# Weight loads in 4 KB source runs, and one packet per transfer and engine, in a fused attention and spectral-mixing kernel

## The chip, the cores and the metric

The kernel runs on one core of one Trainium2 chip. The metric is device time in microseconds (us) of one execution. The kernel before takes 456.14 us, the median of three runs (455.82 to 456.61). The profiled execution has a span of 453.8 us.

## The reference: what is computed

The program is a causal attention followed by a mixing of the sequence's lowest 64 frequencies. Cut to what matters:

```python
# attention: q, k, v are (8 batches, 8 heads, 576 positions, 64), s is (8, 8, 576)
cum    = cumsum(maximum(s, 0), axis=-1)
scores = q @ k.T / 8 + minimum(-(cum[..., :, None] - cum[..., None, :]), 0)   # causal
x      = softmax(scores) @ v                       # as (8, 576, 512)

# spectral mixing: w_r, w_i are (64 modes, 512, 512), w_ch is (512, 512)
X  = rfft(x, axis=1)[:, :64]                       # 64 modes of 512 channels, complex
Yr = einsum('bmd,mde->bme', X.real, w_r) - einsum('bmd,mde->bme', X.imag, w_i)
Yi = einsum('bmd,mde->bme', X.real, w_i) + einsum('bmd,mde->bme', X.imag, w_r)
u  = x + irfft(Yr + 1j * Yi, n=576)
out = u + maximum(u @ w_ch, 0)                     # float32
```

All inputs are float32 in HBM. Each of the 64 modes has a 512 x 512 matrix of its own in `w_r` and in `w_i`, and each is used for only eight rows (the batches). So the weights, 64 x 512 x 512 x 4 bytes x 2 = 134.2 MB, are read once, and q, k and v add 28.3 MB.

## The kernel before: the parts that matter here

The channels are cut into four groups `g` of 128, the modes into eight chunks `c` of eight. A step `n` of the first part is one batch and one pair of heads, 32 steps in all. In each step the scores, the exponentials and the products with v of one pair of heads are made, the forward transform `fft` of the pair before, and (from step 8 on) `modes`, the products of one chunk with its weights. The last group of channels is multiplied after the 32 steps, among the work of the end.

All loads from HBM that change float32 into 16 bits on the way are issued on the GpSimd queue by one helper. A weight tile holds four modes of one chunk, all of them even or all of them odd (`par`), for 128 input channels on the 128 partitions. One row of 512 output channels is one run of 2,048 bytes in HBM and 1,024 bytes in the tile:

```python
t = (wpool, wpool2)[i].tile([P, WM, DM], BF16, name="w_sb", tag="w")   # P=128, WM=4, DM=512
src = (moe_w_r, moe_w_i)[ri]
todo.append((
    t,
    src[c * MC + par : (c + 1) * MC : 2, g * P : (g + 1) * P, :].rearrange("m p e -> p m e"),
))
wt[key] = t
...
def load(*lists):
    todo = [((i + 0.5) / len(l), x) for l in lists for i, x in enumerate(l)]
    for _, (dst, src) in sorted(todo, key=lambda t: t[0]):
        nc.gpsimd.dma_start(out=dst, in_=src)
```

There are 128 weight tiles. The first eight go into tensors that are not used yet; the others share 17 buffers (11 and 6), and 11 of them at the end. Beside them q and k of a step are one transfer each (128 partitions, runs of 2,304 bytes), v is two (runs of 512 bytes), and the last 64 positions of v come in eight transfers (64 partitions, runs of 256 bytes).

The forward transform of a step is five matmuls over the positions, 128 channels on the output's partitions and three times 64 columns (sine, cosine, minus sine of all modes), and two copies into `xs`, where the weights' product finds its stationary operand:

```python
ps = auxpool.tile([P, 3 * NM], FP32, name="ft_ps", tag="aux")      # NM=64 modes
for T in range(NT):                                                 # NT=5
    nc.tensor.matmul(ps, x_all[:nT, g, b, T, :], Ff_sb[:nT, T, :],
                     start=(T == 0), stop=(T == NT - 1))
for ri in range(2):
    nc.vector.tensor_copy(
        out=xs[g % 2][:, 3 - 2 * ri, :, b, :],
        in_=ps[:, (1 - ri) * NM : (3 - ri) * NM].rearrange("p (r m) -> p r m", r=2),
    )
```

`modes` makes the product of a chunk: 16 matmuls, each of 32 stationary columns and 512 moving columns, four side by side on the four quarters of the output's partitions. Of the 32 columns 16 belong to the mode (real and imaginary part of eight batches) and 16 are zero, so that an even and an odd mode share a quarter:

```python
for x in range(4):
    ri, par = divmod(x, 2)
    cols = xs[g % 2].rearrange("p k r b m -> p (k r b) m")
    c0 = (48, 16)[ri] - 16 * par
    if meanwhile and x in meanwhile:
        meanwhile[x]()
    for cg in range(4):
        nc.tensor.matmul(
            ps[32 * cg : 32 * cg + 32, :],
            cols[:, c0 : c0 + 32, c * MC + 2 * cg + par],
            wt[(g, c, ri, par)][:, cg, :],
            start=(x == 0), stop=(x == 3), tile_position=(0, 32 * cg), ...
        )
```

The 16 columns of zeros come from a memset of `xs`. A GpSimd issue also waits for the transfer that was issued eight before it on that queue: the program has eight semaphores for these transfers, taken in turn.

The small rows of sums (`qtA`, `qtB`), the constants and the output go over the SyncE queue and aren't changed.

Of the kernel before, what the change touches and what calls it, by code (L numbers as in the profile page):

```python
# [9 lines left out]
FP32 = mybir.dt.float32  # L10
FP16 = mybir.dt.float16
BF16 = mybir.dt.bfloat16
# [6 lines left out]
def kernel(  # L19
# [11 lines left out]
    nc = tc.nc  # L31
    B, H, S, D = q.shape
    NM = moe_w_r.shape[0]
    DM = H * D
    P = 128
    NT = (S + P - 1) // P
    tails = [min(P, S - T * P) for T in range(NT)]
# [8 lines left out]
    MC = 8  # L46
# [7 lines left out]
    W = 2 * P  # L54
    NWN = S // W
    NK = 2 * NWN


    ident_np = np.eye(P, dtype=np.float32)
# [7 lines left out]
    m_idx = np.arange(NM, dtype=np.float64)  # L67
    ang = 2.0 * np.pi * np.outer(t_idx, m_idx) / S
    Ff_np = np.zeros((SP, 3 * NM), dtype=np.float16)
    Ff_np[:S, :NM] = np.sin(ang)  # L70
    Ff_np[:S, NM : 2 * NM] = np.cos(ang)
    Ff_np[:S, 2 * NM :] = -np.sin(ang)
    cmv = np.where(m_idx == 0, 1.0, 2.0) / S
    G_np = np.zeros((NM, 2, SP), dtype=np.float64)
    G_np[:, 0, :S] = cmv[:, None] * np.cos(ang.T)
# [16 lines left out]
    gp = ctx.enter_context(tc.tile_pool(name="globals", bufs=1))  # L92


    x_all = gp.tile([P, NG, B, NT, P], FP16, name="x_all")
    y_acc = gp.tile([P, NCK, DM], FP32, name="y_acc")

    xs = [gp.tile([P, 5, 2, B, NM], BF16, name=f"xs{i}") for i in range(2)]
    ident16h = gp.tile([P, P], FP16, name="ident16h")
    Ff_sb = gp.tile([P, NT, 3 * NM], FP16, name="Ff_sb")  # L100
    G_sb = gp.tile([P, SP], FP16, name="G_sb")
# [4 lines left out]
    auxpool = ctx.enter_context(tc.tile_pool(name="aux_psum", bufs=2, space=PSUM))  # L106
# [3 lines left out]
    qkpool = at.enter_context(tc.tile_pool(name="qk_sb", bufs=LA + 1))  # L110
    cumt_sb = ap_.tile([P, NK + 1, NPAIR], FP32, name="cumt_sb")
    cumt4 = ap_.tile([P, NPAIR // 2], FP32, name="cumt4")
# [18 lines left out]
    p_sb = [ap_.tile([P, poff[-1]], FP16, name=f"p_sb{i}") for i in range(NP_)]  # L131
    p4 = [ap_.tile([P, P], FP16, name=f"p4_{i}") for i in range(2)]

    temp = xs[1].rearrange("p k r b m -> p (k r b m)").bitcast(FP32)
    ident32, negm32, s_sb = temp[:, :P], temp[:, P : P + 2 * W + NL], temp[:NPAIR, -S:]
    ident16 = ap_.tile([P, P], BF16, name="ident16")
    negm = ap_.tile([P, 2 * W + NL], BF16, name="negm")
# [49 lines left out]
    wt = {}  # L187
# [3 lines left out]
    def ring_of(k):  # L191
        if k < NE:
            return None
        return int(k < LW2 and (k - NE) % (WA + WB) >= WA)

    def loads_w(upto):
        todo = []
        while len(wt) < min(upto, len(wq)):
            g, c, ri, par = key = wq[len(wt)]
            i = ring_of(len(wt))  # L200
            if i is None:
                t = early[len(wt)]
            else:
                t = (wpool, wpool2)[i].tile([P, WM, DM], BF16, name="w_sb", tag="w")
            src = (moe_w_r, moe_w_i)[ri]
            todo.append((
                t,
                src[c * MC + par : (c + 1) * MC : 2, g * P : (g + 1) * P, :].rearrange("m p e -> p m e"),
            ))
            wt[key] = t  # L210
        return todo

    def load(*lists):

        todo = [((i + 0.5) / len(l), x) for l in lists for i, x in enumerate(l)]
        for _, (dst, src) in sorted(todo, key=lambda t: t[0]):
            nc.gpsimd.dma_start(out=dst, in_=src)  # L217

# [7 lines left out]
    for n in range(N):  # L228
# [3 lines left out]
        while nt < min(w, len(wq)):  # L232
            i = ring_of(nt)
# [37 lines left out]
    with tc.tile_pool(name="cum_psum", bufs=1, space=PSUM) as cpsum:  # L271
# [5 lines left out]
            out=cum, data0=spos, data1=zer, initial=0.0, op0=ALU.add, op1=ALU.add  # L277
        )
        nc.vector.tensor_scalar(out=ncum_sb, in0=cum, scalar1=-8.0, scalar2=None, op0=ALU.mult)
        ct_ps = cpsum.tile([P, NK + 1, NPAIR], FP32, name="ct_ps")  # L280
        keys = cum[:, : NF * P].rearrange("c (w p r) -> c w r p", p=P, r=2)
        for x in range(NK):
            nc.tensor.transpose(
# [4 lines left out]
        for x in range(2):  # L288
            nc.vector.tensor_copy(out=tl[:, x, :], in_=cum[:, (NT - 1) * P :])
        nc.tensor.transpose(  # L290
            ct_ps[:, NK, :], tl.rearrange("p x t -> p (x t)"), ident32[:NPAIR, :NPAIR]
        )
        nc.vector.tensor_copy(out=cumt_sb, in_=ct_ps)
        for x in range(2):
            rows = slice(NL * x, NL * x + NL)
            nc.vector.tensor_copy(
                out=cumt4[rows, :], in_=cumt_sb[rows, NK, x::2]
            )

    def pad_p():  # L300
        for i in range(NP_):
            for x in range(NK):
                nc.vector.memset(p_sb[i][:, poff[x] + S - x // 2 * W : poff[x + 1]], 1.0)


    def cum_rows(n):
        if n >= N:
            return
        g, b = divmod(n, B)
        p0 = b * H + 2 * g  # L310
        nc.sync.dma_start(out=qtA[n % NQ][D : D + 1, :], in_=ncum_sb[p0 : p0 + 1, :])
        nc.sync.dma_start(out=qtB[n % NQ][0:1, :], in_=ncum_sb[p0 + 1 : p0 + 2, :])
# [98 lines left out]
    def fft(n):  # L411
        if n < 0:
            return
        g, b = divmod(n, B)
        ps = auxpool.tile([P, 3 * NM], FP32, name="ft_ps", tag="aux")
        for T in range(NT):
            nT = tails[T]
            nc.tensor.matmul(  # L418
                ps,
                x_all[:nT, g, b, T, :],  # L420
                Ff_sb[:nT, T, :],
                start=(T == 0), stop=(T == NT - 1),
            )
        for ri in range(2):
            nc.vector.tensor_copy(
                out=xs[g % 2][:, 3 - 2 * ri, :, b, :],
                in_=ps[:, (1 - ri) * NM : (3 - ri) * NM].rearrange("p (r m) -> p r m", r=2),
            )

    def modes(g, c, meanwhile=None):  # L430


        ps = auxpool.tile([P, DM], FP32, name="yp", tag="aux")
        for x in range(4):
            ri, par = divmod(x, 2)
            cols = xs[g % 2].rearrange("p k r b m -> p (k r b) m")
            c0 = (48, 16)[ri] - 16 * par
            if meanwhile and x in meanwhile:
                meanwhile[x]()
            for cg in range(4):  # L440
                nc.tensor.matmul(  # L441
                    ps[32 * cg : 32 * cg + 32, :],
                    cols[:, c0 : c0 + 32, c * MC + 2 * cg + par],
                    wt[(g, c, ri, par)][:, cg, :],
                    start=(x == 0), stop=(x == 3),
                    tile_position=(0, 32 * cg), skip_group_check=True,
                )
        if g == 0:
            nc.vector.tensor_copy(out=y_acc[:, c, :], in_=ps)
        elif g < NG - 1:  # L450
            nc.vector.tensor_tensor(out=y_acc[:, c, :], in0=ps, in1=y_acc[:, c, :], op=ALU.add)
        else:
            yb = spool.tile([P, DM], FP16, name="y_sb", tag="y")
            for cols in halves if c == NCK - 1 else [slice(0, DM)]:
                nc.vector.tensor_tensor(
                    out=yb[:, cols], in0=ps[:, cols], in1=y_acc[:, c, cols], op=ALU.add
                )
            if c >= NCK - 2:
                spread(c, 0, yb)
            return yb  # L460
# [3 lines left out]
    def spread(c, which, rows):  # L464

        nc.sync.dma_start(out=yv[16 * c : 16 * c + 16, :, which, :], in_=rows)
# [53 lines left out]
    with tc.tile_pool(name="sc_psum", bufs=2, space=PSUM) as scpool, \  # L520
            tc.tile_pool(name="tr_psum", bufs=1, space=PSUM) as trpool, \
            tc.tile_pool(name="av_psum", bufs=1, space=PSUM) as avpool:
        cum_rows(0)
        transposes(0, 0)
        transposes(0, 1)
        load(loads_qkv(2))
        pad_p()
        for n in range(N):
            if n in (0, 2):
                nc.vector.memset(xs[n // 2].rearrange("p k r b m -> p (k r b m)").bitcast(FP32), 0.0)  # L530
            tails_due = loads_tails(n // B + 1)[n % B - 3 : n % B - 2] if 2 < n % B < 5 else []
            load(loads_qkv(n + LA) + tails_due, loads_w(on_chip[n]))
            cum_rows(n + 1)
            scores(n, 0)
            av(n - 1, 1)
            transposes(n + 1, 0)
            scores(n, 1)
            i = first_pairs[n - N + len(first_pairs)] if n >= N - len(first_pairs) else None
            if i is not None:
                first_transposed(i, 0)  # L540
            transposes(n + 1, 1)
            fft(n - 1)
            av(n, 0)
            if i is not None:
                first_product(i, 0)
                first_transposed(i, 1)
            for c in mode_steps.get(n, []):
                modes(c // NCK, c % NCK)
            if i is not None:
                first_product(i, 1)  # L550
            if n == N // 2:
                nc.gpsimd.dma_start(out=wch_sb, in_=moe_w_ch.rearrange("(dt p) e -> p dt e", p=P))
        av(N - 1, 1)
        fft(N - 1)
# [10 lines left out]
    zpool = ctx.enter_context(tc.tile_pool(name="z_psum", bufs=2, space=PSUM))  # L565

    NLOC = 4
    old = xs[0].rearrange("p k r b m -> p (k r b m)")
    xt_sb = [
        old[:, i * 2 * DM : (i + 1) * 2 * DM].bitcast(FP16).rearrange("p (x t c) -> p x t c", x=2, c=P)  # L570
        for i in range(2)
# [199 lines left out]
    c = NCK - 2  # L771
# [21 lines left out]
    for x in range(2):  # L793
        dts = slice(x * DT // 2, (x + 1) * DT // 2)
        ps = auxpool.tile([P, DT // 2, P], FP16, name="yt_ps", tag="aux")
# [88 lines left out]
```

The softmax here doesn't subtract the row's maximum and nothing guards it: scores larger than these inputs give would overflow.

## Time and profile before

| what | before |
| --- | --- |
| time, median of 3 | 456.14 us |
| span of the profiled execution | 453.8 us |
| busy: PE / DVE / ACT / POOL | 340.4 / 241.0 / 221.9 / 183.0 us |
| GpSimd queue: packets, bytes written | 98,960, 81.81 MB |
| weight transfers: issues, KB written each | 128, 512 KB |
| weight transfer, issue to landing | 11.9 us (median) |
| GpSimd issue of a weight transfer | 0.75 us |
| forward transform: 5 matmuls, one after the other | 0.75 us |
| copy of a transform (two in a step) | 277 ns each |

How to read it: PE is TensorE, DVE is VectorE, ACT is ScalarE, POOL is GpSimd, SP is SyncE. The GB/s of the profile count the bytes that are written; where a load turns float32 into 16 bits, twice as many are read from HBM. A "packet" of the profile's DMA queues is one run moved by one of the 16 DMA engines, or one write of a semaphore. The chain is the path of waits and work that ended last, followed back from the last instruction.

### The profile page before, as it was taken

The numbers are of one execution on the slowest core, as the hardware profiler recorded it, in microseconds if no ns is written. First come the engines' busy times: TensorE is split into PE (matmuls) and PEld (weight loads), VectorE is DVE, ScalarE is ACT, GpSimd is POOL, SyncE is SP. The second block draws the span as 40 slices with busy tenths as digits, with TensorE's granted clock in tenths as the row PEclk, the third lists the DMA queues.
The fourth block names the chain that finished last, engine by engine and source line by source line (L and its number), as shares of the span: only waits on it lengthen the run. The fifth ranks groups of instructions, "written<-read, shape, count | busy, mean of one in ns | idle before, by whom it ended". The sixth has DMA issues, their size and how long they took to land.

```text
span 453.8 us, 10370 instructions
## 1 busy us (share of the span) xinstructions
PE 340.4 (75%) x4233; PEld 218.6 (48%) x4265; DVE 241.0 (53%) x535; ACT 221.9 (49%) x390; POOL 183.0 (40%) x269
## 2 busy tenths in 40 slices
PE   1779887976563979836677857688889678879995
PEld 1456665654342656624445535456554335534332
DVE  7775665753242656723436434446655443562796
ACT  1585877464242656724435444455551323431774
POOL 6655554554344565434364444444433231200000
PEclk9996999998576889968878899889996986999999
DMA  9999999999999999999999999999999999995688
GB/s 176 200 203 203 202 201 204 202 204 204 205 204 202 201 203 202 205 205 204 202 196 203 204 204 203 204 203 202 206 207 208 207 206 206 207 214 109 232 298 317
DMA packets 108511, 93.75 MB, mean 207 GB/s; under 512 B 28384, under 2 KB 103648, under 8 KB 108464
## 3 DMA queue, kind: packets, MB, share of 16 engines
q0 software_dynamic: 98960, 81.81, 113.8%
q1 hardware_dynamic: 9504, 11.29, 7.8%
q8 instruction: 33, 0.54, 0.4%
q14 instruction: 14, 0.11, 0.1%
HBM read 164.56 MB, written 9.44 MB: 383 GB/s over the span
## 4 chain that ended last, share of the span: by engine, by line
DMA 51%; PE 31%; DVE 8%; issue 4%; POOL 2%; ACT 2%; SPq 0%; DVEq 0%; POOLq 0%; ACTq 0%
DMA w_sb<-in_moe_w_i_dram 21%; DMA q<-in_q_dram 15%; DMA w_sb<-in_moe_w_r_dram 11%; PE sc_ps L365 4%; PE av_ps L394 4%; PE z_ps L602 3%; PE yp L441 3%; PE sc_ps L359 3%; PE tr_ps L324 3%; DMA k<-in_k_dram 2%; PE z_ps L693 2%; PE g_ps L652 2%; PE ft_ps L418 2%; PE u_ps L712 2%; PE u_ps L693 1%
## 5 line engine op out<-in xcount | busy, mean ns | idle before, releaser
L373 ACT ACTIVATE p_sb<-sc_ps,cumt_sb 128x576 f16<-128x576 f32 (+1 forms) x256 | 141.7, 635 | 45.6 <-PE sc_ps L365 45.0
L217 POOL DMA_DIRECT2D w_sb<-in_moe_w_i_dram x60 | 45.1, 751 | 85.0 <-PE yp L441 37.6
L217 POOL DMA_DIRECT2D w_sb<-in_moe_w_r_dram x60 | 45.3, 757 | 63.5 <-DMA w_sb<-in_moe_w_r_dram 28.2
L217 POOL DMA_DIRECT2D v<-in_v_dram x72 | 50.8, 708 | 32.0 <-DMA w_sb<-in_moe_w_r_dram 7.4
L324 PE MATMUL tr_ps<-ident,q 64*64 64x64 bf16 x576 | 17.5, 210 | 54.3 <-DMA q<-in_q_dram 54.3
L359 PE MATMUL sc_ps<-negm,ident 128*128 128x256 bf16 x256 | 55.5, 303 | 0.2
L327 DVE COPY qtA<-tr_ps 64x576 bf16<-64x576 bf16 x32 | 23.8, 743 | 49.6 <-PE tr_ps L324 49.5
L441 PE MATMUL yp<-w_sb,xs 128*32 128x512 bf16 x480 | 36.5, 406 | 14.1 <-DMA w_sb<-in_moe_w_i_dram 11.1
L344 ACT ACTIVATE p<-sc_ps,cumt 128x64 f16<-128x64 f32 x32 | 10.0, 313 | 74.3 <-PE sc_ps L340 74.3
L394 PE MATMUL av_ps<-v,p_sb 128*128 128x65 f16 x1024 | 44.5, 198 | 0.0
L394 PEld LDWEIGHTS <-p_sb 128*128 128x128 f16 x1024 | 39.5, 100 | 4.9 <-issue 0.8
L327 DVE COPY ktA<-tr_ps 64x576 bf16<-64x576 bf16 x32 | 24.0, 749 | 33.6 <-PE tr_ps L324 33.6
L324 PEld LDWEIGHTS <-q 64*64 64x64 bf16 x576 | 13.7, 123 | 57.0 <-DMA q<-in_q_dram 56.3
L365 PE MATMUL sc_ps<-qtB,ktB 128*128 128x64 bf16 (+2 forms) x160 | 34.9, 324 | 3.5 <-issue 2.4
L365 PE MATMUL sc_ps<-qtA,ktA 65*128 65x512 bf16 (+2 forms) x192 | 36.5, 299 | 0.7 <-DMA qtA<-ncum_sb 0.7
L399 DVE TENSOR_REDUCE den<-av_ps 128x5 f32<-128x10 f32 x64 | 10.8, 169 | 49.1 <-PE av_ps L394 48.9
L441 PEld LDWEIGHTS <-xs 128*32 128x32 bf16 x512 | 22.6, 170 | 23.8 <-issue 19.8
L404 DVE TENSOR_TENSOR x_all<-av_ps,rcp 128x320 f16<-128x320 f32 x64 | 31.5, 491 | 2.2
L327 ACT COPY ktB<-tr_ps 64x576 bf16<-64x576 bf16 x32 | 20.3, 634 | 20.3 <-DVE ktA L327 19.4
L365 PEld LDWEIGHTS <-ktB 128*128 128x128 bf16 x192 | 22.4, 117 | 14.8 <-issue 6.3
L324 PE MATMUL tr_ps<-ident,k 64*64 64x64 bf16 x576 | 17.3, 209 | 15.3 <-DVE qtB L327 10.7
L602 PE MATMUL z_ps<-wch_sb,xs 128*128 128x512 f16 x96 | 26.1, 421 | 0.2 <-DVE xs L596 0.2
(117 smaller groups left out, 534.8 us busy)
## 6 DMA issues: line engine op xcount, KB each, us to landing
w_sb<-in_moe_w_r_dram POOLq DMA_DIRECT2D x60, 512.0 KB, 11.9
w_sb<-in_moe_w_i_dram POOLq DMA_DIRECT2D x60, 512.0 KB, 11.9
q<-in_q_dram POOLq DMA_DIRECT2D x32, 144.0 KB, 9.9
k<-in_k_dram POOLq DMA_DIRECT2D x32, 144.0 KB, 10.0
v<-in_v_dram POOLq DMA_DIRECT2D x72, 64.0 KB, 9.7
out_dram<-r_sb SPq DMA_DIRECT2D x16, 256.0 KB, 2.2
out_dram<-r_w SPq DMA_DIRECT2D x16, 256.0 KB, 2.6
x_all<-in_moe_w_i_dram POOLq DMA_DIRECT2D x3, 512.0 KB, 9.9
```

What stands on the lines that cost most here:

```text
L217: nc.gpsimd.dma_start(out=dst, in_=src)
L324: nc.tensor.transpose(ps[rows, r, :], src[rows, r, :], ident16[rows, rows])
L327: copy(out=dst[n % NQ][rows, :].rearrange("d (p r) -> d p r", r=R), in_=ps[rows].rearrange("d r p -> d p r"),)
L359: nc.tensor.matmul(ps[:, bass.ds(w * S, W)], ident16, negm[:, bass.ts(r, W)], start=True, stop=False, skip_group_check=True,)
L365: nc.tensor.matmul(ps[:, c0 : c0 + i1 - i0], keys[:, w, r, :], qt[:, i0:i1], start=False, stop=True, skip_group_check=True,)
L373: nc.scalar.activation(out=pt[:, poff[x] : poff[x] + S - w * W], in_=ps[:, w * S : (w + 1) * S - w * W], func=ACTF.Exp, bias=cumt_sb[:, x, ...
L394: nc.tensor.matmul(ps[:, I, r : r + NCH], lhsT, rhs, start=(i == 0), stop=(i == len(todo) - 1), skip_group_check=True,)
L399: nc.vector.tensor_reduce(out=den, in_=ps[:, :, 0 : VW : NCH], axis=mybir.AxisListType.X, op=ALU.add)
L404: nc.vector.tensor_tensor(out=x_all[:, g, b, :, D * h : D * h + D], in0=ps[:, :, 1 : NCH], in1=rcp.unsqueeze(2).to_broadcast([P, NT, D]), ...
L441: nc.tensor.matmul(ps[32 * cg : 32 * cg + 32, :], cols[:, c0 : c0 + 32, c * MC + 2 * cg + par], wt[(g, c, ri, par)][:, cg, :], start=(x == ...
L602: nc.tensor.matmul(z[:, x, :], xts[i][:, x, dt, :], wch_sb[:, dt, :], start=(dt == 0), stop=(last and dt == DT - 1), skip_group_check=True,)
L693: nc.tensor.matmul(dst[x][r, :], G_sb[rows, bass.ds(T * P, r.stop - r.start)], yv[rows, bb, which, :], start=start, stop=True, skip_group_ ...
```

## The change

It has three parts that belong together. First, a weight tile is loaded in runs of 4,096 bytes in place of 2,048: two neighbouring input channels of one mode lie side by side in HBM, so a partition now takes two neighbouring channels. The 128 channels of one mode then fill 64 partitions, and two modes share a tile, the even one on the lower half of the partitions, the odd one on the upper half. Each half is a transfer of its own, so a tile takes two transfers. Second, as the contraction now runs over 64 partitions with two channels each (`q`), the forward transform has to deliver its results in that order: each of its matmuls is cut in four (channels by `q`, modes by half), its copies in two, and the zeros in `xs` move from columns to partitions. Third, every load of the helper asks for a single packet per transfer and engine. The purpose is to spend less time per run on the DMA engines.

The core of the diff (cuts marked with ...):

```diff
-    xs = [gp.tile([P, 5, 2, B, NM], BF16, name=f"xs{i}") for i in range(2)]
+    xs = [gp.tile([P, 2, 2, 2, 2, B, HM], BF16, name=f"xs{i}") for i in range(2)]   # HM=32, HP=64
 ...
-            todo.append((
-                t,
-                src[c * MC + par : (c + 1) * MC : 2, g * P : (g + 1) * P, :].rearrange("m p e -> p m e"),
-            ))
+            m0 = c * MC + par * MC // 2
+            for h in range(2):
+                todo.append((
+                    t[HP * h : HP * h + HP].rearrange("p (m q) e -> p m (q e)", q=2),
+                    src[m0 + h : m0 + MC // 2 : 2, g * P : (g + 1) * P, :].rearrange(
+                        "m (p q) e -> p m (q e)", q=2
+                    ),
+                ))
 ...
-            nc.gpsimd.dma_start(out=dst, in_=src)
+            nc.gpsimd.dma_start(out=dst, in_=src, single_packet=True)
 ...
-        ps = auxpool.tile([P, 3 * NM], FP32, name="ft_ps", tag="aux")
-        for T in range(NT):
-            nT = tails[T]
-            nc.tensor.matmul(ps, x_all[:nT, g, b, T, :], Ff_sb[:nT, T, :], ...)
-        for ri in range(2):
-            nc.vector.tensor_copy(...)
+        ps = auxpool.tile([P, 2, 3 * HM], FP32, name="ft_ps", tag="aux")
+        for q_ in range(2):
+            for T in range(NT):
+                nT = tails[T]
+                for h in range(2):
+                    nc.tensor.matmul(
+                        ps[HP * h : HP * h + HP, q_, :],
+                        x_all[:nT, g, b, T, q_::2],
+                        Ff_sb[:nT, T, 3 * HM * h : 3 * HM * (h + 1)],
+                        start=(T == 0), stop=(T == NT - 1),
+                        tile_position=(0, HP * h), skip_group_check=True,
+                    )
+        for h in range(2):
+            rows = slice(HP * h, HP * h + HP)
+            for k in range(2):
+                nc.vector.tensor_copy(
+                    out=xs[g % 2][rows, :, k, h, :, b, :],
+                    in_=ps[rows, :, k * HM : (k + 2) * HM].rearrange("p q (r m) -> p q r m", r=2),
+                )
 ...
+        def product(ri, q_, cg):
             nc.tensor.matmul(
                 ps[32 * cg : 32 * cg + 32, :],
-                cols[:, c0 : c0 + 32, c * MC + 2 * cg + par],
-                wt[(g, c, ri, par)][:, cg, :],
-                start=(x == 0), stop=(x == 3),
+                cols[:, q_, 1 - ri, :, c * MC // 2 + cg],
+                wt[(g, c, ri, cg // 2)][:, 2 * (cg % 2) + q_, :],
+                start=(ri == 0 and q_ == 0), stop=(ri == 1 and q_ == 1),
                 tile_position=(0, 32 * cg), skip_group_check=True,
             )
         for x in range(4):
-            ri, par = divmod(x, 2)
+            ri, y = divmod(x, 2)
             if meanwhile and x in meanwhile:
                 meanwhile[x]()
-            for cg in range(4):
-                ...
+            for z in range(4):
+                if meanwhile:
+                    product(ri, z // 2, 2 * y + z % 2)
+                else:
+                    product(ri, y, z)
```

Number and shape of the products in `modes` stay as they were: 16 of 32 by 512 per chunk. In the last chunk, the one with `meanwhile`, the order goes tile by tile; in the others both tiles of a pair are needed from the first product on.

More of the change, by code (lines that the diff above doesn't have):

```diff
@@ L56 @@
     NK = 2 * NWN
+    HM = NM // 2
+    HP = P // 2
     ident_np = np.eye(P, dtype=np.float32)
@@ L69 @@
     Ff_np = np.zeros((SP, 3 * NM), dtype=np.float16)
-    Ff_np[:S, :NM] = np.sin(ang)
-    Ff_np[:S, NM : 2 * NM] = np.cos(ang)
-    Ff_np[:S, 2 * NM :] = -np.sin(ang)
+    for h in range(2):
+        for i, f in enumerate((np.sin(ang), np.cos(ang), -np.sin(ang))):
+            Ff_np[:S, (3 * h + i) * HM : (3 * h + i + 1) * HM] = f[:, h::2]
     cmv = np.where(m_idx == 0, 1.0, 2.0) / S
@@ L96 @@
     y_acc = gp.tile([P, NCK, DM], FP32, name="y_acc")
-    xs = [gp.tile([P, 5, 2, B, NM], BF16, name=f"xs{i}") for i in range(2)]
+    xs = [gp.tile([P, 2, 2, 2, 2, B, HM], BF16, name=f"xs{i}") for i in range(2)]
+    xs_flat = [t.rearrange("p q k h r b m -> p (q k h r b m)") for t in xs]
     ident16h = gp.tile([P, P], FP16, name="ident16h")
@@ L132 @@
     p4 = [ap_.tile([P, P], FP16, name=f"p4_{i}") for i in range(2)]
-    temp = xs[1].rearrange("p k r b m -> p (k r b m)").bitcast(FP32)
+    temp = xs_flat[1].bitcast(FP32)
     ident32, negm32, s_sb = temp[:, :P], temp[:, P : P + 2 * W + NL], temp[:NPAIR, -S:]
@@ L414, in fft @@
         g, b = divmod(n, B)
-        ps = auxpool.tile([P, 3 * NM], FP32, name="ft_ps", tag="aux")
-        for T in range(NT):
-            nT = tails[T]
[L418 to L423, printed above, removed]
-        for ri in range(2):
[L425 to L428, printed above, removed]
+        ps = auxpool.tile([P, 2, 3 * HM], FP32, name="ft_ps", tag="aux")
@@ L430, in modes @@
+        for h in range(2):
+            rows = slice(HP * h, HP * h + HP)
[4 more added lines that the diff above has]
+                )
     def modes(g, c, meanwhile=None):
         ps = auxpool.tile([P, DM], FP32, name="yp", tag="aux")
+        cols = xs[g % 2].rearrange("p q k h r b m -> p q k (h r b) m")
@@ L434, in modes @@
+        def product(ri, q_, cg):
+            nc.tensor.matmul(
+                ps[32 * cg : 32 * cg + 32, :],
+                cols[:, q_, 1 - ri, :, c * MC // 2 + cg],
+                wt[(g, c, ri, cg // 2)][:, 2 * (cg % 2) + q_, :],
+                start=(ri == 0 and q_ == 0), stop=(ri == 1 and q_ == 1),
+                tile_position=(0, 32 * cg), skip_group_check=True,
+            )
         for x in range(4):
-            ri, par = divmod(x, 2)
-            cols = xs[g % 2].rearrange("p k r b m -> p (k r b) m")
@@ L437, in modes @@
-            c0 = (48, 16)[ri] - 16 * par
+            ri, y = divmod(x, 2)
             if meanwhile and x in meanwhile:
                 meanwhile[x]()
-            for cg in range(4):
-                nc.tensor.matmul(
-                    ps[32 * cg : 32 * cg + 32, :],
-                    cols[:, c0 : c0 + 32, c * MC + 2 * cg + par],
-                    wt[(g, c, ri, par)][:, cg, :],
-                    start=(x == 0), stop=(x == 3),
-                    tile_position=(0, 32 * cg), skip_group_check=True,
-                )
+            for z in range(4):
[3 more added lines that the diff above has]
+                    product(ri, y, z)
@@ L529 @@
             if n in (0, 2):
-                nc.vector.memset(xs[n // 2].rearrange("p k r b m -> p (k r b m)").bitcast(FP32), 0.0)
+                nc.vector.memset(xs_flat[n // 2].bitcast(FP32), 0.0)
             tails_due = loads_tails(n // B + 1)[n % B - 3 : n % B - 2] if 2 < n % B < 5 else []
@@ L567 @@
     NLOC = 4
-    old = xs[0].rearrange("p k r b m -> p (k r b m)")
+    old = xs_flat[0]
     xt_sb = [
```

## The prediction, made before the changed kernel was run

> **What bounds the kernel now.** I read the page's DMA lines first, then the windows, the chain, and last the waits of GpSimd.
>
> ```profile
> GB/s 176 200 203 203 202 201 204 202 204 204 205 204 202 201 203 202 205 205 204 202 196 203 204 204 203 204 203 202 206 207 208 207 206 206 207 214 109 232 298 317
> DMA packets 108511, 93.75 MB, mean 207 GB/s; under 512 B 28384, under 2 KB 103648, under 8 KB 108464
> q0 software_dynamic: 98960, 81.81, 113.8%
> HBM read 164.56 MB, written 9.44 MB: 383 GB/s over the span
> ```
>
> The rate hardly moves from the second slice of the page to the 36th: 200 to 208 GB/s written, so about 405 GB/s read, while the work on the other engines changes from attention to projections. A rate so flat under changing work is a ceiling of the transfers, not of those who use them. The windows view (time, busy us and count of PE, PEld, DVE, ACT, POOL, granted clock, DMA share, GB/s) gives the rate by stage, and where it ends:
>
> ```profile
> 100.00:340.00 240.00, 169.57 (x2376) 116.11 (x2398) 111.41 (x261) 115.47 (x219) 110.31 (x160) 0.85 1.29 203
> 380.00:410.00 30.00, 25.39 (x232) 14.89 (x230) 17.40 (x26) 11.29 (x17) 4.45 (x6) 0.95 1.24 209
> 412.00:414.00 2.00, 2.00 (x13) 0.77 (x11) 0.00 (x0) 0.00 (x0) 0.00 (x0) 1.00 0.73 144
> ```
>
> The mixed stage (weights, q, k, v) gets 203, the stage with weights alone 209, and the loads end at about 414. So 412 of 454 us are one long load, and 40 us of products and output follow. The chain says the same:
>
> ```profile
> DMA 51%; PE 31%; DVE 8%; issue 4%; POOL 2%; ACT 2%; SPq 0%; DVEq 0%; POOLq 0%; ACTq 0%
> 353.00 19.81 DMA w_sb<-in_moe_w_i_dram
> 372.85 0.59 PE yp L441 x4
> 391.97 0.70 DVE y_sb L455
> ```
>
> The last DMA wait on it ends at 372.8; from there it is PE and DVE work to the end. What the loads save before 373 should therefore come off the end, what they save later need not.
>
> ```profile
> POOL w_sb L217 <- PE yp L441: 43.8, 15, 9.9
> POOL w_sb L217 <- DMA w_sb<-in_moe_w_r_dram: 32.5, 19, 2.5
> POOL w_sb L217 <- DMA w_sb<-in_moe_w_i_dram: 32.2, 19, 2.1
> w_sb<-in_moe_w_r_dram POOLq DMA_DIRECT2D x60, 512.0 KB, 11.9
> ```
>
> GpSimd waits in turn for an earlier transfer (eight may be open) and for a buffer that a product frees. Even the longest of these waits, 9.9 us, left no dip in the rate, since 12 us of transfers are queued.
>
> **What the Trainium skill says.** (1) "DMA: Bandwidth & Descriptors", section "Where 436 GB/s comes from": 16 engines x 32 bytes x 850 MHz = 435.2 GB/s. The trace agrees as a ceiling: the weight stage reads 2 x 209 = 418, the mixed one 406. (2) Same page, "Why small descriptors are slow (HBM only)": about three cycles are lost per packet, and joining runs is worth it only at 256 bytes or less. The trace agrees with the first: a weight run takes 16 x 1,024 B / 209 GB/s = 78.4 ns, its 64 beats at 850 MHz 75.3 ns, so 3.1 ns are lost, 2.6 cycles. The second I doubt, as 3.1 ns times 65,536 runs aren't nothing. (3) Same page, "Queues, rings and completion order": an engine turns to another queue only at the end of a packet. No trace here has long packets. (4) Same page, "Rules for kernel authors": two transfers to halves of the partitions serialize, one whole transfer is advised. Nothing in this trace shows weights on half the partitions.
>
> **The change part by part.**
>
> *Room there is.* 164.56 MB at 435.2 GB/s take 378 us; the stage takes 412. Of the 34 us some 4 are start and end (75 GB/s in the first 4 us, 144 in the last 2). The other 30 us over 98,960 packets on 16 engines are 4.9 ns per packet: 3.1 for weight runs, more for the small ones and for the semaphore writes.
>
> *4 KB runs.* 128 tiles x 512 = 65,536 runs become 32,768. Saved: 32,768 x 3.1 ns / 16 = 6.3 us.
>
> *One packet.* The other 32,768 weight runs still lose 32,768 x 3.1 / 16 = 6.3 us, and the 28,672 runs of q, k and v 28,672 x 4.9 / 16 = 8.8 us. If the loss is one per packet, all 15 us go; if it is one per run, none. I choose three quarters, 11.5 us: the loss per run is about the same for runs of very different length, which looks like a fixed gap of the kind that packets are there to close.
>
> *More transfers.* 128 more, each with one semaphore write per engine; the packet records of the trace give 22 ns for one. 128 x 22 ns = 2.8 us back.
>
> Sum for the load stage: 6.3 + 11.5 - 2.8 = 15 us. Of it 373/414, 90%, lie ahead of the last DMA wait of the chain: 13.5 us.
>
> *GpSimd.* 128 issues more. The runs of a half tile are as many as those of q (128), which takes 0.57 us to issue against 0.75 for a weight tile: 256 x 0.57 - 128 x 0.75 = +50 us, to some 230 of 454. Still not the bound.
>
> *Forward transform.* Five matmuls in 0.75 us become 20 with half the columns. Eighteen transposes of 64 columns take 0.69 us, 17 products with v 0.73, so 38 to 43 ns each, and 20 take about 0.85 us: +0.1 us. The copies go from 2 x 277 to 4 x about 277 ns: +0.55 us on a DVE busy to 53%. In the steady stage PE waits for q anyway (54 us in all), and this is hidden. Only in the stretch from 20 to 67 us, where PE is about 90% busy, I count 8 steps x 0.12 = 1 us. In the last chunk two quarters at a time work in place of four; 16 products took 1.1 us, so about +0.4 us.
>
> Total: 13.5 - 1.4 = 12.1 us off 456.1: **444 us**.
>
> **The rivals.**
>
> *The loss is per run, not per packet.* Then only 6.3 - 2.8 = 3.5 us of load time are gained, less the 1.4: about 454. For it: the skill's remark that joining helps only short runs. Against it: nothing that I can see.
>
> *The write side becomes the limit.* A half tile is written to 64 partitions, perhaps through half of the ways into the memory. Those would have to carry the whole rate of 210 GB/s. If they stall at, say, 5% less, the stage grows by about 20 us and the result is near 470. Against it: the engines needn't be at the same half at the same time.
>
> *Less is queued.* Eight open transfers now hold about half the bytes: at the end 8 x 512 KB written were 20 us of work (the 19.81 above), and 10 will be left. The one wait of 9.9 us for a buffer then has nothing to spare, and the engines may run dry for a few microseconds; in the steady stage 12 become about 8 against waits of mostly 2 to 3. I give it 0 to 4 us, more probably near 0, as the chain there is PE work.
>
> *Long packets hold up SyncE's queue.* The rows for `qtA` take 4.6 us now; behind packets of 32 KB per engine (1.2 us each) perhaps 7. They are issued more than a step ahead (6.3 us in the fastest stretch), so I expect little.
>
> *All loss goes and more.* At 435 the stage would take about 385 us and the kernel 432.
>
> **Range and chances.** The lower end is nearly all the loss gone, 433; the upper is the per-run rival with 1 us of new gaps, 455. Faster by over 2% needs less than 447.0, that is 9 of the 12 us: I give it 0.60. Within 2%, mainly the per-run rival: 0.32. Slower, the write side: 0.08.
>
> **What would show it.** Right: the mixed stage at 210 to 214 GB/s in place of 203 and the weight stage at 213 or more in place of 209; loads over by about 399; DMA's share of the chain smaller and the tail after the last load still 40 us; `w_sb` landing 6 to 9 us after issue; POOL busy near 230 us. The per-run rival: 205 and 212. The write side: below 203, most clearly where only weights are loaded. Too few queued: slices of the page with a dip before 400. A wait of `sc_ps` for `qtA` by many microseconds would show SyncE's queue held up. The prediction fails most easily on the share of 15 us that the packets give back, which no view of this trace shows.

## The result, and the profile after

The changed kernel takes 453.38 us (median of four runs, 452.77 to 454.39), the kernel before in the same runs 455.98 us. The ratio is 0.9942, with a 95% interval of 0.9925 to 0.9958: faster by about 2.6 us where 12 had been predicted, at the upper end of the range.

The page of the changed kernel, the lines of the transfers and the chain's shares by engine:

```profile
GB/s 182 200 204 206 204 204 205 205 207 207 207 207 201 196 192 200 208 207 207 204 203 207 208 205 207 207 205 203 207 210 211 209 209 209 210 218 91 236 299 316
DMA packets 77796, 93.83 MB, mean 208 GB/s; under 512 B 30432, under 2 KB 40160, under 8 KB 77744
...
q0 software_dynamic: 68240, 81.81, 104.8%
...
DMA 48%; PE 33%; DVE 9%; issue 5%; POOL 2%; ACT 2%; SPq 0%; DVEq 0%; POOLq 0%; ACTq 0%
...
w_sb<-in_moe_w_r_dram POOLq DMA_DIRECT2D x120, 256.0 KB, 8.0
```

The same bytes go in 30,720 fewer packets (98,960 to 68,240: 32,768 runs fewer, 2,048 semaphore writes more). The rate is up by only 1 to 3 GB/s in most slices, and slices 13 to 16 have a dip (201, 196, 192, 200) that the kernel before did not have. The windows by stage (stretch, its length, then busy us and instructions of PE, PEld, DVE, ACT and POOL; granted clock, DMA share and GB/s; the share counts overlapping packets and can pass 1):

```profile
100.00:340.00 240.00, 187.72 (x2758) 124.60 (x2755) 123.37 (x307) 117.31 (x221) 144.32 (x236) 0.83 1.19 205
340.00:380.00 40.00, 30.43 (x244) 16.87 (x243) 18.36 (x30) 10.24 (x14) 18.82 (x32) 0.79 1.12 210
...
410.00:412.00 2.00, 2.00 (x12) 0.85 (x12) 0.00 (x0) 0.00 (x0) 0.00 (x0) 1.00 0.40 93
```

The kernel before, with weights alone:

```profile
340.00:380.00 40.00, 30.38 (x227) 16.57 (x229) 17.08 (x26) 9.18 (x12) 11.85 (x16) 0.79 1.24 207
```

The mixed stage gets 205 GB/s (203 before), the weights alone 210 (207 before in the same window), and the loads end at about 411 in place of 414. On the chain, the last wait for a transfer, and the product behind it:

```profile
360.06 9.96 DMA w_sb<-in_moe_w_i_dram
370.06 1.09 PE yp L449 x5
```

It ends at 370.0 in place of 372.8. The remaining 81 us are as long as before: what was gained by this point, loads and transform together, is the whole gain. The chain's share by engine says less: for DMA it is 51% before and 48% after, but 62% in before_sp below, which takes the time of before.

### The profile page after: what moved, and what is told of

Its sections match the earlier page's. It is cut to its first block, busy times and chain, and to the rows that moved or that the text cites. A ratio compares the mean times of both kernels' runs of the same rounds, so it can differ in the third digit from the quotient of the medians.

```text
span 451.0 us, 11579 instructions
## 1 busy us (share of the span) xinstructions
PE 359.5 (80%) x4745; PEld 226.5 (50%) x4745; DVE 257.3 (57%) x599; ACT 222.1 (49%) x390; POOL 241.2 (53%) x397
## 3 DMA queue, kind: packets, MB, share of 16 engines
q0 software_dynamic: 68240, 81.81, 104.8%
## 4 chain that ended last, share of the span: by engine, by line
DMA 48%; PE 33%; DVE 9%; issue 5%; POOL 2%; ACT 2%; SPq 0%; DVEq 0%; POOLq 0%; ACTq 0%
DMA w_sb<-in_moe_w_i_dram 21%; DMA w_sb<-in_moe_w_r_dram 14%; DMA q<-in_q_dram 5%; PE av_ps L401 4%; PE sc_ps L372 4%; DMA k<-in_k_dram 3%; PE yp L449 3%; PE ft_ps L427 3%; PE sc_ps L366 3%; PE tr_ps L331 2%; PE z_ps L620 2%; PE z_ps L711 2%; DMA wch_sb<-in_moe_w_ch_dram 2%; DVE qtB L334 2%; PE g_ps L670 2%
## 5 line engine op out<-in xcount | busy, mean ns | idle before, releaser
L224 POOL DMA_DIRECT2D w_sb<-in_moe_w_r_dram x120 | 71.5, 596 | 60.4 <-DMA w_sb<-in_moe_w_r_dram 20.0
L224 POOL DMA_DIRECT2D w_sb<-in_moe_w_i_dram x120 | 71.5, 597 | 47.6 <-DMA w_sb<-in_moe_w_i_dram 21.5
L366 PE MATMUL sc_ps<-negm,ident 128*128 128x256 bf16 x256 | 57.2, 310 | 0.2
L449 PE MATMUL yp<-w_sb,xs 128*32 128x512 bf16 x480 | 37.9, 421 | 12.1 <-DMA w_sb<-in_moe_w_i_dram 7.2
L401 PE MATMUL av_ps<-v,p_sb 128*128 128x65 f16 x1024 | 45.8, 200 | 0.0
L372 PE MATMUL sc_ps<-qtB,ktB 128*128 128x512 bf16 (+2 forms) x192 | 42.9, 339 | 0.0
L372 PE MATMUL sc_ps<-qtA,ktA 65*128 65x512 bf16 (+2 forms) x192 | 39.2, 316 | 0.4 <-DMA qtA<-ncum_sb 0.4
L437 DVE CAST xs<-ft_ps 64x128 bf16<-64x128 f32 x128 | 31.4, 284 | 9.4 <-PE ft_ps L427 9.0
L427 PE MATMUL ft_ps<-Ff_sb,x_all 128*64 128x96 f16 (+1 forms) x640 | 34.1, 229 | 1.0 <-DVE x_all L411 1.0
L449 PEld LDWEIGHTS <-xs 128*32 128x32 bf16 x512 | 19.2, 145 | 23.8 <-issue 9.6
L331 PEld LDWEIGHTS <-q 64*64 64x64 bf16 x576 | 13.5, 121 | 35.1 <-DMA q<-in_q_dram 33.9
```

The source lines that it names most:

```text
L224: nc.gpsimd.dma_start(out=dst, in_=src, single_packet=True)
L331: nc.tensor.transpose(ps[rows, r, :], src[rows, r, :], ident16[rows, rows])
L366: nc.tensor.matmul(ps[:, bass.ds(w * S, W)], ident16, negm[:, bass.ts(r, W)], start=True, stop=False, skip_group_check=True,)
L372: nc.tensor.matmul(ps[:, c0 : c0 + i1 - i0], keys[:, w, r, :], qt[:, i0:i1], start=False, stop=True, skip_group_check=True,)
L401: nc.tensor.matmul(ps[:, I, r : r + NCH], lhsT, rhs, start=(i == 0), stop=(i == len(todo) - 1), skip_group_check=True,)
L427: nc.tensor.matmul(ps[HP * h : HP * h + HP, q_, :], x_all[:nT, g, b, T, q_::2], Ff_sb[:nT, T, 3 * HM * h : 3 * HM * (h + 1)], start=(T == ...
```

## The experiments

Two theories. **Per run**: a DMA engine loses a fixed time for every run it moves, whatever packet the run lies in, and some for every transfer. **Per packet**, the one the prediction was built on: the loss is one per packet, and long packets remove it. A third question is what the dearer transform costs. All ratios are against the kernel before, on the same chip.

**One packet alone (before_sp) and the change without it (after_nosp).**

```diff
 # before_sp: the kernel before
-            nc.gpsimd.dma_start(out=dst, in_=src)
+            nc.gpsimd.dma_start(out=dst, in_=src, single_packet=True)
 # after_nosp: the changed kernel, the same line the other way round
```

> The kernel before with one packet per transfer and engine, nothing else changed. If the loss on the DMA engines is one per run whatever packet it lies in (the theory I now hold): 456 us as before, 203 GB/s in the mixed stage and 209 with weights alone. If it is one per packet (the rival that the prediction was built on): 208 and 214 GB/s, 445 us.

> The changed kernel without the single packet. Loss per run: the same as the changed kernel, 453.4 us within 1 us, 205 GB/s in the mixed stage. Loss per packet: back by several microseconds, 457 or more, 203 GB/s. If the long packets did harm (they hold up SyncE's queue): faster than the changed kernel, 451 to 452.

Measured: 455.76 us, ratio 0.9999 (0.999 to 1.0008), and 453.25 us, ratio 0.9937 (0.9923 to 0.9951). The windows of before_sp:

```profile
100.00:340.00 240.00, 173.92 (x2396) 116.92 (x2396) 110.58 (x260) 115.77 (x219) 110.26 (x160) 0.85 1.28 203
...
380.00:410.00 30.00, 25.38 (x234) 15.32 (x231) 17.62 (x27) 11.30 (x17) 4.45 (x6) 0.94 1.24 209
```

203 and 209, to the digit the rates of before. Asking for one packet does nothing here, in either layout. The profile cannot say whether the engines really joined the runs: it still lists 98,960 packets for before_sp, so its packet is a run. The rows of SyncE's queue, which a long packet should have held up, landed after 4.6 us as before.

**The two halves of the change apart (loads_only, compute_only).**

```diff
 # loads_only: the kernel before, with the loads of the change
-            todo.append((t, src[c * MC + par : (c + 1) * MC : 2, ...].rearrange("m p e -> p m e")))
+            m0 = c * MC + par * MC // 2
+            for h in range(2):
+                todo.append((t[HP * h : HP * h + HP]..., src[m0 + h : m0 + MC // 2 : 2, ...]...))   # and single_packet=True
 # compute_only: the changed kernel, with the loads of the kernel before
```

> The changed loads (4 KB runs, two transfers per tile, one packet) with the transform and the products of the kernel before, which then multiply weights that lie in another order: it leaves out the reordering of the channels, so its output differs, but every instruction of the other engines is that of before. If the dearer transform takes part of the gain back: 448 to 450 us. If the loads themselves gain little and the transform costs nothing: 453 us.

> The changed transform (20 matmuls, 4 copies) and order of products with the loads of before: the weights lie in another order than the products take them in, so its output differs. If the transform costs time (2 us up to step 8 and something at low granted clocks after it): 458 to 460 us. If it is hidden behind the loads: 456 us.

Measured: 452.48 us, ratio 0.9928 (0.9916 to 0.9941), and 457.49 us, ratio 1.0032 (1.0021 to 1.0044). The loads alone gain 3.5 us, between the two expectations and nearer the small one; the transform with its order of products costs 1.5 us. Added up they give 2.0 us, against 2.6 for the whole change. Over the changed loads the transform costs less, 453.4 - 452.5 = 0.9 us. Either way the loads themselves brought little: 3.5 us of the 13.5 that the prediction gave them.

**What a run and a transfer cost (runs8k_128, runs4k_128, halves2k).** Three kernels in which only the weight loads differ from before:

```diff
 # runs8k_128: 128 runs of 8 KB, one transfer
+    (t.rearrange("p q e -> p (q e)"), src[c * MC + 4 * par + g].rearrange("(p q) e -> p (q e)", q=4))
 # runs4k_128: 256 runs of 4 KB, one transfer
+    (t.rearrange("p (m q) e -> p m (q e)", q=2),
+     src[m0 : m0 + 2, (g // 2) * 2 * P : (g // 2 + 1) * 2 * P, :].rearrange("m (p q) e -> p m (q e)", q=2))
 # halves2k: 512 runs of 2 KB, two transfers of 64 partitions
+    for h in range(2): (t[rows], src[c * MC + par : (c + 1) * MC : 2, g * P + rows.start : g * P + rows.stop, :]...)
```

> The kernel before with each weight tile read as 128 runs of 8 KB, one per partition, in one transfer (a whole mode, four channels to a partition); the products take the tile as before, so the weights are in another order and the output differs. Theory (4.0 ns lost per run and 24 ns per transfer on each engine, solved from the weight stages of before and after): 49,152 runs fewer, 12 us of load time, nine tenths of it on the path: 445 us, and about 213 GB/s written where weights alone are loaded. Rival (the memory gives no more than some 416 GB/s read): 208 to 209 GB/s there and 451 us or more.

> The kernel before with each weight tile read as 256 runs of 4 KB in one transfer to all 128 partitions (two modes, 256 channels); the order of the weights differs, so the output does. Theory: 32,768 runs fewer at the same number of transfers, 8.2 us of load time, 448.5 us, 211 GB/s with weights alone. If the doubled transfers cost nothing: the same as the changed loads alone, 452.5 us and 208 GB/s.

> The kernel before with each weight tile in two transfers of 64 partitions each, runs of 2 KB as before, and the same result. Theory: 128 transfers more at 24 ns per engine, 3.1 us: 459 us, 206 to 207 GB/s with weights alone. If writing to half of the partitions is itself slower: 205 or less there, 462 us or more. If a transfer costs nothing: 456 us.

Measured: 445.67 us (ratio 0.9776, 0.976 to 0.9792), 449.07 us (0.9846, 0.9833 to 0.9859) and 458.69 us (1.0066, 1.0051 to 1.0082), each within 0.7 us of the per-run theory. The GB/s lines of the three pages, runs8k_128 first; slices 30 to 35 are the stage with weights alone:

```profile
GB/s 176 204 208 208 206 206 208 207 209 211 210 210 208 206 208 204 211 211 209 207 203 210 210 209 210 211 208 206 214 214 215 213 214 214 214 222 90 236 304 315
```

```profile
GB/s 175 202 206 207 204 204 207 206 208 208 208 208 205 203 196 202 209 209 207 206 204 207 208 208 208 208 206 206 211 211 213 211 211 211 211 219 102 237 302 315
```

```profile
GB/s 176 198 201 202 201 200 201 202 203 202 203 203 199 197 198 201 204 203 203 201 184 202 203 202 203 203 202 201 203 206 206 205 205 205 205 213 122 228 295 317
```

About 214, 211 and 205, against 207 before and 209 to 210 after the change: the order that runs and transfers ask for. To put figures to it, I took in each trace the 80 us from the end of the last packet of q, k or v on, in which the GpSimd queue moves weights alone, and counted the packet records per engine. "Loss" is what is left of the 80 us after all bytes moved in them (for weights those read from HBM) at 435.2 GB/s. This is the ceiling that the prediction took from the Trainium skill, "DMA: Bandwidth & Descriptors", section "Where 436 GB/s comes from", which states it for the ports of the on-chip memory. No run here reached it, and it serves as a yardstick only: the differences between the rows hardly depend on it.

| kernel | run; transfers for 512 KB | runs | transfers | loss us |
| --- | --- | --- | --- | --- |
| halves2k | 2 KB; 2, to 64 partitions | 993 | 62 | 4.95 |
| before | 2 KB; 1, to 128 | 1,001 | 31 | 4.36 |
| after | 4 KB; 2, to 64 | 507 | 63 | 3.34 |
| runs4k_128 | 4 KB; 1, to 128 | 512 | 32 | 2.64 |
| pairs (below) | 4 KB; 1, to 64 | 512 | 32 | 2.64 |
| runs8k_128 | 8 KB; 1, to 128 | 259 | 32 | 1.76 |

From 2 to 4 KB (before to runs4k_128) 489 runs fewer save 1.72 us, from 4 to 8 KB 253 fewer save 0.88 us: **3.5 ns per run** both times. From before to halves2k 31 transfers more cost 0.59 us, from runs4k_128 to the change 31 more cost 0.70 us: **about 20 ns per transfer and engine**. Starting the stretch up to 6 us later, or ending it after 60 us, leaves 3.3 to 3.6 ns and 17 to 23 ns. Whether the engine or the memory that it reads loses the time of a run is not shown; a longer run is longer for both.

The write side, a rival of the prediction, is refuted as a limit: pairs fills half of the partitions with each transfer and loses what runs4k_128 loses. The 2.6 us of halves2k are those of its 128 more transfers.

**A cheaper transform (ft10, ft_short), and its copies (after_act, copies2).**

```diff
 # ft10: 10 matmuls of 256 columns (sin, cos, cos, -sin of even and odd modes) in place of 20 of 96
+    nc.tensor.matmul(ps[HP * q_ : HP * q_ + HP, :], x_all[:nT, g, b, T, q_::2], Ff_sb[:nT, T, :], ...)
 # ft_short: 12 of 20 left out        -  for T in range(NT):        +  for T in (0, NT - 1):
 # copies2: two of four left out      -  for k in range(2):         +  for k in range(1):
 # after_act                          -  nc.vector.tensor_copy(     +  (nc.vector.tensor_copy, nc.scalar.copy)[h](
```

> The changed kernel with its transform in 10 matmuls of 256 columns in place of 20 of 96; both modes' halves come out of one matmul, and the four copies move the upper partitions to where they belong. The result is the same. If it is PE's share of the dearer transform that costs 1.5 us: 452 us, chunk 0 at 79 us into the kernel in place of 80.7. If it is the two copies more on DVE: no better than 453.4.

> The changed kernel with 12 of the 20 matmuls of each transform left out (three of the five blocks of positions, so the output differs); the copies stay. The transform then takes less of PE than that of before (8 matmuls, about 0.4 us, against 0.75). If PE's share costs the 1.5 us: 452 us or less. If it is hidden: 453.4 us.

> The changed kernel with two of its four transform copies (those of the odd modes) on ScalarE in place of VectorE; the result is the same. If the 1.5 us of the dearer transform come from VectorE's queue, where two copies more (0.57 us a step) delay the copies of q and k: 452 us or less, first product at about 79 us. If they come from PE's 20 matmuls or from the wait for the last copy: 453.4 us, unchanged. ScalarE itself in the way: slower.

> The changed kernel with two of the four transform copies left out (the other half of the transform's results then stays zero, so the output differs). VectorE's share of the 1.5 us: 452 us if it is nearly all of it. PE's share: 453.4 us, unchanged.

Measured: ft10 454.80 us (ratio 0.9974, 0.9963 to 0.9986), ft_short 452.77 (0.9922, 0.9903 to 0.994), after_act 453.40 (0.995, 0.9932 to 0.9967), copies2 453.55 (0.9949, 0.9931 to 0.9966). The copies do not matter: neither moving nor dropping two of them changed the time. Leaving out PE work gave a little, but the interval overlaps that of the change itself. More could not be expected: these kernels start from the change, where the transform costs 0.9 us. after_act has its first product of weights at 79.1 us, as expected for a gain, where the change has it at 80.7, and takes no less time: where the first product lies does not alone decide the time. ft10 came out slower than the change although its transform is shorter (0.79 us a step against 0.91, from the chain), with the first product at 80.9 us. Of the 2.0 us between the two profiles 1.0 lies behind VectorE's last sum (which ends at 448.2 and 447.1 us, spans 453.0 and 451.0), among the writes of the output. Why is not shown, and ft10 is no clean test of PE's share.

**The order of the products (order_tile).**

```diff
-                if meanwhile:
-                    product(ri, z // 2, 2 * y + z % 2)
-                else:
-                    product(ri, y, z)
+                product(ri, z // 2, 2 * y + z % 2)
```

> The changed kernel with the products of every chunk taken tile by tile, as the last chunk does it already, so that the first products need one tile only; the result is the same. If the order costs the 1.5 us (one tile more has to land first, and 6 to 10 products in place of 4 follow the last landing): 452 to 452.5 us. If not: 453.4, or some tenths more as two quarters work at a time.

Measured: 453.56 us, ratio 0.9937 (0.9919 to 0.9956): no difference. So of the 1.5 us that compute_only shows, neither the copies nor the order alone is the cause. PE's matmuls are left, and not shown: ft_short is too close to the change to say so, and ft10 too mixed.

**Fewer transfers at the same runs (pairs, pairs_act, pairs2).** The theory says that a version with 4 KB runs and half the transfers should be faster than the change. Two tiles are held side by side in one buffer, and a transfer fills half the partitions of both:

```diff
-    t = (wpool, wpool2)[i].tile([P, WM, DM], BF16, name="w_sb", tag="w")       # WA, WB = 11, 6
+    t = (wpool, wpool2)[i].tile([P, 2 * WM, DM], BF16, name="w_sb", tag="w")   # WA, WB = 6, 3
+    for h in range(2):
+        (t[HP * h : HP * h + HP]..., src[c * MC + h : (c + 1) * MC : 2, ...]...)   # four modes in a transfer
 # pairs, pairs_act: weights asked for earlier, W0 = 4 in place of 3, on_chip[-1] + 6 in place of + 5
 # pairs_act: and the copies of odd modes on ScalarE, as in after_act
 # pairs2: pairs, with W0 = 2 in place of 4 and on_chip[-1] + 4 in place of + 6 (weights asked for later)
```

> The changed kernel with its two tiles of a chunk held side by side in one buffer, so that one transfer brings all four even modes to the lower half of the partitions and one all four odd modes to the upper half: runs of 4 KB as before, but 130 weight transfers in place of 256; buffers for 18 tiles (nine pairs) in place of 17. The result is the same. Theory (24 to 34 ns per transfer on each engine): 126 transfers fewer, 3 to 4 us of load time, 450 us. If the coarser buffers cost more than that: 453 us or above. If a transfer costs nothing: 453.4.

> The same with the copies of the odd modes on ScalarE. If both causes hold, the gains add: 448.5 to 449 us, near the 449.1 of 4 KB runs with the transform of before. If the copies don't matter: as the pairs alone, 450 us.

> The kernel with paired tiles, its weight loads now scheduled no further ahead than in the kernel before (two tiles at the start in place of four, at most four new tiles a step asked for in place of six). If the order of the loads had eaten the gain: first product at about 80 us in place of 85.7, 450.5 us. If the coarser buffers are the reason: 453 to 454 us as without it.

Measured: 453.79 us (0.9952, 0.9933 to 0.9971), 454.30 us (0.9967, 0.9952 to 0.9982) and 453.52 us (0.9933, 0.9912 to 0.9954). None beats the change. Here the GB/s lines of pairs and then of pairs2:

```profile
GB/s 183 200 203 205 205 177 197 208 206 209 208 208 208 174 203 207 207 209 209 208 195 206 208 206 209 209 206 207 209 212 212 211 211 211 212 217 63 232 300 316
```

```profile
GB/s 176 200 206 206 205 205 206 207 206 208 208 208 207 205 191 205 208 209 208 205 205 208 209 204 207 208 209 207 211 211 212 211 211 211 211 213 52 235 301 315
```

The stage with weights alone is at 211 to 212, as fast as in runs4k_128: the transfers do cost what the theory says. But pairs has holes at 177 and 174. In both stretches GpSimd is issuing mostly `q`, `k` and `v`, and waits mainly for earlier transfers (at most 2.7 us a time), so small transfers take most of the eight open places. This is what the trace shows beside the holes; their cause was not isolated. Buffers come free later than in the change, too. From GpSimd's waits over the whole of pairs (sum, number, longest, us):

```profile
POOL w_sb L235 <- PE yp L460: 24.0, 6, 9.3
```

and from PE's timeline of pairs, its first product of weights (start and length, us):

```profile
85.72 0.87 PE L460 MATMUL yp<-y_acc,xs 128*32 128x512 bf16 x10 [0.36 <-DVE xs L448]
```

The change has 3.0 us of such waits for a buffer, and its first product at 80.7. But the kernel before has 43.8 us of them and no hole, so such a wait is not a loss by itself. Asking for the weights later (pairs2) closed the first hole and brought the first product to 81.6, but the time stayed. In its profile the work of gathering and projecting between chunks 3 and 4, which waits for no load, took 15.7 us (371.1 to 386.9) against 14.5 in the change and 15.3 in the kernel before. Whether that is more than a difference between executions was not tried. What 4 KB runs with few transfers can give is known from runs4k_128; how to get it with the right order of weights is not.

## Why the prediction was wrong, by its own steps

That 453.4 us lies within the range of 433 to 455 is no merit of the mechanism: the upper end had been drawn for the per-run rival.

*Where the bound lies*: right. The kernel is one load of 411 us, the chain's last wait for a transfer moved by as much as the time did, and the tail after the load kept its 40 us.

*4 KB runs*: right in its mechanism and a little low. The term was 6.3 us at 3.1 ns per run; at the measured 3.5 it is 32,768 x 3.5 / 16 = 7.2 us. The 3.1 came from the 209 GB/s of 380 to 410 us, taken for weights alone. By the packet records 8.7 GB/s of it are SyncE's (`yv` from `y_sb` and `v_sb`), which change no type and so read no more than they write. In 340 to 380 us, where SyncE moves 0.8, the rate is 207, and the same working gives 3.9 ns, with the transfer's share in it.

*One packet*: this is the step that failed. "I choose three quarters, 11.5 us" stands in the sum, and the runs show 0 (ratio 0.9999). The argument for it was that runs of different length lose about the same; that fits a loss per run as well, and the prediction's first rival said so. Nor did it follow from the prediction's own figures: 30 us on 16 engines less 65,536 x 3.1 ns leave 8.3 ns for each of the 33,424 other packets, not 3.1 (and three quarters of 15.1 are 11.3). I wrote "Against it: nothing that I can see", and should have given the rival more than the 0.32 of "within 2%": a loss per packet and a loss per run can't be told apart in a profile that lists each run as a packet. The Trainium skill ("DMA: Bandwidth & Descriptors", section "Why small descriptors are slow (HBM only)") says that joining descriptors into packets pays only at 256 bytes or less. That was the better guide: before_sp gained nothing, though whether its packets were joined is not shown. The about three cycles that the same section gives for a packet are 3.5 ns at 850 MHz, and this is what each run lost here. Lengthening the runs themselves is another matter: 2 to 4 to 8 KB gave 7 us and 3.4 us more in runs4k_128 and runs8k_128.

*More transfers*: right. 2.8 us predicted, halves2k shows 2.6, and 128 x 20 ns are 2.6.

*The transform*: 1.4 us predicted, 1.5 measured by compute_only. The place looks right too. PE's first product of weights, in loads_only and then in compute_only:

```profile
78.56 0.91 PE L447 MATMUL yp<-y_acc,xs 128*32 128x512 bf16 x12
79.62 0.87 PE L445 MATMUL yp<-y_acc,xs 128*32 128x512 bf16 x10 [0.36 <-DVE xs L433]
```

Before it is at 78.7, so the new loads alone do not move it, and the transform alone moves it by 0.9 us where 1 us was counted. With both it is at 80.7, and at 80.1 in after_nosp. That the time follows from this is not shown, as after_act says.

*GpSimd*: right. 241 us busy for 230, 0.60 us for a half tile, and no bound.

With the measured sizes the sum is (7.2 + 0 - 2.6) x 0.9 - 1.5 = 2.6 us, as measured. So close a match is partly luck: by the same sum loads_only should have gained 4.1 us, and it gained 3.5.

*The rivals.* The per-run one came true, with 205 GB/s in the mixed stage; its 212 with weights alone were 210. The write side is refuted by pairs and halves2k. Too little queued: the dip of slices 13 to 16 fits it in part. It is in loads_only too (201, 192, 195, 200), whose other work is that of before, so the transform does not make it; in runs8k_128, where whole tiles are queued, it is nearly gone. But half tiles do not make it alone: runs4k_128 and pairs2, with 512 KB in a transfer, fall to 196 and 191, and halves2k, with half tiles of 2 KB runs, only to 197. Against 207 around it, the dip costs the change about 2 us. A busy PE alone does not make it either: in 140 to 150 us the rate is 191 with PE 62% busy, in 150 to 160 it is 203 with PE 94% busy. The cause stays open. SyncE's queue was hardly held up, and not by long packets: `qtA` took 4.9 us in place of 4.6, and 5.0 in after_nosp.

## What to carry to other kernels

Where the page shows a flat rate below the ceiling of the engines, count runs and transfers: here a run cost 3.5 ns and a transfer about 20 ns on each engine, which says in advance what a new layout can give. Lengthening runs paid up to 8 KB, but splitting the transfer to get there gave a third back (2.6 of 7.2 us); keep the number of transfers when you lengthen the runs. A loss "per item" must be tested on the cheapest edit first: one argument of one line (before_sp) would have taken some 10 of the 12 predicted microseconds (11.5 x 0.9) out of the sum.

## What the runs showed of the hardware that was not expected

The request for one packet per transfer and engine changed nothing that the profile or the time can show, neither with 2 KB runs (0.9999) nor with 4 KB (0.9937 without against 0.9942 with). Runs of 8 KB raised the rate again, to 214 GB/s written and so 428 read, with one core at work. Loads to 64 partitions ran no slower than to 128 (a loss of 2.64 us in 80 us for pairs and for runs4k_128) beyond the cost of the extra transfers.
